# A fused layer norm, local attention and GeGLU kernel: three tiles transposed by DMA, late weights requested from GpSimd, the load order and a buffer count changed

## Chip, cores and metric

The kernel runs on one core of a Trainium2 chip. The metric is the device time of one execution in microseconds (us); it is given as a median over executions. One execution was also profiled, and its trace holds every instruction's start and end, in us from the start of the span.

## What is computed

The input x is 2048 rows of 512 numbers in bf16. Two branches read the same normalized rows, and their product is added back to x:

```python
xn = _layernorm(x, axis=-1)
s = _A_ref(xn, A_wqkv, A_wo)
g = _silu(_B_ref(xn, B_w_gate, B_w_up, B_w_down))
return x + s * g
```

Branch A is an attention of 32 heads of 16 numbers, in which position p sees only the eight positions p, p-2, ..., p-14; positions before the start are masked out. It ends in a product with wo (512 x 512). Branch B is a gated unit: gelu(xn w_gate) * (xn w_up) is multiplied by w_down, with an inner width of 1792.

## The kernel before

**Tiling.** The 2048 rows are 16 tiles of 128 rows (128 is the number of partitions), grouped in four chunks of four tiles: chunk 0 is tiles 0 to 3, chunk 1 tiles 4 to 7, and so on. All matmuls need the normalized rows with the 512 features on the partitions, so each normalized tile `xn` (L197 `normalize`) is transposed into `xnT` of its chunk. There are two ways to do that. `transpose` (L204) issues four TensorE transposes into a PSUM buffer, which ACT (or VectorE) copies to xnT. `transpose_by_dma` (L229) issues four DMA transposes of 128 x 128 from SP's queue.

**Stages.** For each chunk j the program runs three stages: `qkv` (L252; twelve blocks of 128 output features, four each of q, k and v), `glu` (L389; 14 steps fc, each with four matmuls into g_ps, four into u_ps, two evictions on ACT and the product h on VectorE) and `down` (L402; per tile 14 matmuls into y_ps with wd, four into s_ps with wo, and the closing product and sum). The order of program is: qkv of chunk 0, then for each chunk its glu, the qkv of the next chunk, and its down stage. The work of the attention is put between the steps of these stages: products of q and shifted k (`qk_product`, L285, VectorE), their sums (`logits`, L293, TensorE, with Exp on ACT and, for chunk 0, seven memsets of E on GpSimd), products with v (`av_product`, L353, VectorE; tile name pv), their sums (`av_sums`, L364, TensorE; o_ps), the denominators (L313), and the division (`divide`, L379, VectorE; oT).

**What sets the order.** The program is scheduled by hand. `at(key, fn, *args)` (L436) hangs a call on a step, and `run` (L439) issues the calls of a step ahead of it, in the order in which they were hung. Each engine then takes its own instructions strictly in program order, and waits on semaphores for what it needs from others. So a call's place fixes its place in each queue that it uses: TensorE (PE), VectorE (DVE), ScalarE (ACT), GpSimd (POOL), and SP, from which all DMAs of the kernel before are issued.

**Loads.** At the start SP requests x tiles 0 to 3 one by one, the q, k and v thirds of wqkv, then the rest of x between the halves of w_gate and w_up (L94 to L102). `load_late_weights` (L104) requests wd (w_down, 1792 KB) and wo (four requests of 128 KB). It hangs on step 0 of chunk 0's glu stage, behind the DMA transposes of tile 7 and `load_v` (L270; the four requests of v_arr for chunk 0, which read back from DRAM what the v blocks wrote there).

**Chunk 1's tiles.** Tiles 4 to 7 are normalized in chunk 0's qkv stage. Tiles 4, 5 and 6 are transposed on TensorE at steps 0, 1 and 2 of chunk 0's glu stage, and tile 7 by DMA. Chunk 1's qkv stage, which follows that glu stage, is the first to read them.

**Chunk 2's tiles.** Their statistics (`moments`, L187) come at steps 7 to 10 of that glu stage and their normalization at steps 8 to 11. `moments` ends with a power on GpSimd (L193, rstd to the power -0.5) that `normalize` waits for. Logits come at step 9, and the first two pv at steps 12 and 13.

**Buffers.** xn lives in pool `sm4`, four buffers per name. The PSUM pool `mm` has four buffers, which g_ps, u_ps, qkv_ps, y_ps, s_ps and the transposes' tr take in turn.

**Start.** Before x arrives, TensorE runs 17 matmuls of 256 columns on zeros (`warm_up`, L221), and twice four of 128 columns between the first transposes.

Of the kernel before, what the change touches and what calls it, by code (L numbers as in the profile page):

```python
# [10 lines left out]
BF16 = mybir.dt.bfloat16  # L11
F32 = mybir.dt.float32

P = 128
# [14 lines left out]
def kernel(  # L29
# [13 lines left out]
    nc = tc.nc  # L43
    B, S, D = A_x.shape
    DF = B_w_gate.shape[1]
    NT, NC, NF, NJ = S // P, D // P, DF // P, S // TQ
    TPQ = TQ // P
# [5 lines left out]
    def pool(name, bufs, **kw):  # L53
        return ctx.enter_context(tc.tile_pool(name=name, bufs=bufs, **kw))
# [11 lines left out]
    sm = pool("sm", 3)  # L66
    sm2 = pool("sm2", 2)
    sm4 = pool("sm4", 4)
    dram = pool("dram", 1, space=bass.MemoryType.DRAM)
    mm = pool("mm", 4, space=bass.MemoryType.PSUM)  # L70
    att = pool("att", 1, space=bass.MemoryType.PSUM)
# [3 lines left out]
    wqkv_sb = wts.tile([P, NC, 3 * D], BF16, name="wqkv_sb")  # L75
    wg_sb = wts.tile([P, NC, DF], BF16, name="wg_sb")
    wu_sb = wts.tile([P, NC, DF], BF16, name="wu_sb")
    wd_sb = wts.tile([P, NF, D], BF16, name="wd_sb")
# [4 lines left out]
    def load_x(t, n=1):  # L83
        nc.sync.dma_start(
            out=x_sb[:, t : t + n, :],
            in_=x2d[t * P : (t + n) * P, :].rearrange("(t p) d -> p t d", p=P),
        )

    def load_w(dst, src, lo, hi):
        nc.sync.dma_start(  # L90
            out=dst[:, :, lo:hi], in_=src.rearrange("(k p) n -> p k n", p=P)[:, :, lo:hi]
        )

    for t in range(TPQ):  # L94
        load_x(t)
    for i in range(3):
        load_w(wqkv_sb, A_wqkv, i * D, (i + 1) * D)
    load_x(TPQ, TPQ)
    for i, (lo, hi) in enumerate(((0, DF // 2), (DF // 2, DF))):
# [2 lines left out]
        load_x((2 + i) * TPQ, TPQ)  # L102

    def load_late_weights():  # L104
        nc.sync.dma_start(out=wd_sb[:], in_=B_w_down.rearrange("(k p) n -> p k n", p=P))
        for g in range(NC):
            nc.sync.dma_start(
                out=wo_sb[:, g, :],
                in_=bass.AP(
                    tensor=A_wo.tensor, offset=g * 4 * D, ap=[[D, 4], [DH * D, H], [1, D]]  # L110
                ),
            )
# [7 lines left out]
        out=vT.rearrange("(k p) n -> p k n", p=P)[:, :, 0:PAD],  # L120
        in_=warm[:, 0 : NC * PAD].rearrange("p (k n) -> p k n", k=NC),
# [54 lines left out]
    def first_moments(t):  # L176
        nc.vector.bn_stats(out=stats[:, t, :], in_=x_sb[:, t, :])  # L177
        nc.vector.bn_aggr(out=mv[:, t, :], in_=stats[:, t, :])
        nc.scalar.activation(
            out=std[:, t, :], in_=mv[:, t, 1:2], func=AF.Sqrt, bias=epsc[:], scale=1.0  # L180
        )

    def first_normalize(t):
        nc.vector.reciprocal(out=rstd[:, t, :], in_=std[:, t, :])
        normalize(t)
# [9 lines left out]
    xns = {}  # L195

    def normalize(t):  # L197
        xn = xns[t] = sm4.tile([P, D], BF16, name="xn")
        nc.vector.tensor_scalar(
            out=xn[:], in0=x_sb[:, t, :], scalar1=mv[:, t, 0:1], scalar2=rstd[:, t, :],  # L200
            op0=ALU.subtract, op1=ALU.mult,
        )
# [18 lines left out]
    def warm_up(n, cols):  # L221

        ps = mm.tile([P, TQ], F32, name="warm_ps", tag="mm")
        for _ in range(n):
            nc.tensor.matmul(
                ps[:, 0:cols], lhsT=warm[:, 0:P], rhs=warm[:, 0:cols], start=True, stop=True
            )
# [24 lines left out]
    def qkv(j, fo, i0=0, n=TQ, ps=None):  # L252
        which, c = divmod(fo, NC)
        if fo == 0 and i0 == 0:
            st[j]["q"] = qp.tile([P, NC, TQ], BF16, name="q_sb")
        if ps is None:
            ps = mm.tile([P, n], F32, name="qkv_ps", tag="mm")[:]
            project(ps, wqkv_sb, fo * P, j, i0, n)
        if which == 0:
            nc.scalar.activation(out=st[j]["q"][:, c, i0 : i0 + n], in_=ps, func=AF.Copy)  # L260
        elif which == 1:
            lo = PAD + j * TQ + i0
            nc.scalar.activation(out=k_sb[:, c, lo : lo + n], in_=ps, func=AF.Copy)  # L263
        else:
            vst = sm4.tile([P, TQ], BF16, name="vst")
            nc.scalar.activation(out=vst[:], in_=ps, func=AF.Copy)  # L266
            lo = PAD + j * TQ
            nc.sync.dma_start(out=vT[c * P : (c + 1) * P, lo : lo + TQ], in_=vst[:])
# [167 lines left out]
    def at(key, fn, *args):  # L436
        side.setdefault(key, []).append((fn, args))
# [5 lines left out]
    for i in range(TPQ):  # L443
        at(("qkv", 0, i), normalize, TPQ + i)
        at(("glu", 0, 7 + i), moments, 2 * TPQ + i)
        if i < TPQ - 1:
            at(("glu", 0, i), transpose, TPQ + i)
        at(("glu", 0, 8 + i), normalize, 2 * TPQ + i)
        at(("glu", 1, 0), transpose_by_dma, 2 * TPQ + i)
        at(("glu", 1, 10 + i), moments, 3 * TPQ + i)  # L450
        at(("qkv", 2, 2 * i), normalize, 3 * TPQ + i)
        at(("glu", 2, 0), transpose_by_dma, 3 * TPQ + i)
# [31 lines left out]
    HT = TPQ // 2  # L484
    HQ = HT * P
    warm_up(17, TQ // 2)
    first_moments(0)
    first_moments(1)
    first_normalize(0)
# [27 lines left out]
    for i in range(NC):  # L517
        run("qkv", 0, i)
        run("qkv", 0, NC + i)
        qkv(0, 2 * NC + i)  # L520
    at(("glu", 0, 0), transpose_by_dma, 2 * TPQ - 1)
    at(("glu", 0, 0), load_v, 0)
    at(("glu", 0, 0), load_late_weights)
    for j in range(NJ):
        for fc in range(NF):
            run("glu", j, fc)
# [36 lines left out]
```

The softmax here doesn't subtract the row's maximum and nothing guards it: scores larger than these inputs give would overflow.

## Time and profile before

| | us |
|---|---|
| median of 3 runs | 230.64 (230.31 to 230.83) |
| the profiled execution | 230.49 |
| its span, first to last instruction | 228.8 |
| PE busy | 222.7 |
| VectorE (DVE) busy | 147.6 |
| ScalarE (ACT) busy | 130.6 |
| GpSimd (POOL) busy | 21.7 |

The page of a profile gives the busy time of each engine and the chain of work that ended last, followed back from the last instruction. In a timeline, a line has the start and the time from the start of its first to the end of its last instruction, the engine, the line of the code, the operation, out<-in by the program's names, the shape and the count; in brackets stand the idle time of the engine before it and what released it. A matmul's end is modelled and overlaps the next, so PE is best read by starts. SPq is SP's issuing of DMAs: its time is that of the request, not of the data. L12 is line 12 of the kernel before; the changed kernel's lines stand up to six further down.

### The profile page before, as it was taken

The page shows a single profiled execution, that of the slowest core. Times are in us where ns is not written, and L with a number is a line of the kernel's source. Part 1 is how long each engine was busy: PE and PEld are TensorE (multiplying, and loading weights), DVE is VectorE, ACT ScalarE, POOL GpSimd, SP SyncE. Part 2 cuts the span into 40 slices and gives each one's busy share as a digit, 9 for nine tenths or more (in the row PEclk, how much of TensorE's full clock was granted, in tenths as well). Part 3 has the DMA queues.
Part 4 walks back from the last instruction along what each step waited for, and adds up shares of the span by engine and source line. Part 5 has one row for each costly group of instructions (what it writes and reads, how often), then busy time and mean ns, then how long its engine had stood idle before and what let it go on. Part 6 is the DMA issues. An engine that isn't in the chain of part 4 may idle for free.

```text
span 228.8 us, 3516 instructions
## 1 busy us (share of the span) xinstructions
PE 222.7 (97%) x1303; PEld 106.8 (47%) x1323; DVE 147.6 (65%) x234; ACT 130.6 (57%) x215; POOL 21.7 (10%) x61
## 2 busy tenths in 40 slices
PE   7999999999999999999999999999999999999994
PEld 5865444444444444444444444444444444444453
DVE  4593996894898198865678169735449429845232
ACT  3679779764514867476721687646741387647211
POOL 1048944100000000110000000000000000000000
PEclk9999999999999999999999999999999999999999
DMA  6999599922366611110266711110038910000001
GB/s 157 357 375 376 140 175 199 315 98 80 91 153 152 135 23 29 27 29 0 92 162 152 162 29 23 26 34 6 30 104 193 202 30 3 0 0 4 23 23 46
DMA packets 29857, 24.33 MB, mean 106 GB/s; under 512 B 9488, under 2 KB 29840, under 8 KB 29840
## 3 DMA queue, kind: packets, MB, share of 16 engines
q1 hardware_dynamic: 29840, 24.11, 41.0%
q8 instruction: 10, 0.16, 0.3%
q14 instruction: 7, 0.06, 0.1%
HBM read 18.61 MB, written 4.31 MB: 100 GB/s over the span
## 4 chain that ended last, share of the span: by engine, by line
PE 94%; ACT 2%; DVE 1%; DMA 1%; issue 1%; ACTq 0%; DVEq 0%
PE y_ps L411 21%; PE u_ps L242 21%; PE g_ps L242 20%; PE qkv_ps L242 17%; PE s_ps L421 6%; PE L_ps L299 3%; PE o_ps L370 3%; DMA x_sb<-in_A_x_dram 1%; PE q_ps L242 1%; PE tr L208 1%; DVE stats L177 1%; ACT L395 1%; ACT u L397 1%; PE den_ps L319 0%; ACT xnT L217 0%
## 5 line engine op out<-in xcount | busy, mean ns | idle before, releaser
L242 PE MATMUL u_ps<-xnT,wu_sb 128*128 128x512 bf16 x223 | 57.3, 379 | 0.2
L242 PE MATMUL g_ps<-xnT,wg_sb 128*128 128x512 bf16 x214 | 56.5, 379 | 0.6 <-issue 0.2
L411 PE MATMUL y_ps<-wd_sb,h 128*128 128x512 bf16 (+1 forms) x234 | 50.9, 366 | 0.2
L399 DVE TENSOR_TENSOR h<-ge,u 128x512 bf16<-128x512 bf16 x56 | 23.8, 424 | 37.5 <-ACT u L397 36.8
L288 DVE TENSOR_TENSOR pk<-q_sb,k_sb 128x2048 bf16<-128x2048 bf16 x32 | 37.8, 1221 | 7.0 <-ACT k_sb L263 7.0
L395 ACT ACTIVATE ge<-g_ps 128x512 bf16<-128x512 f32 x56 | 33.6, 600 | 14.7 <-PE g_ps L242 14.0
L397 ACT ACTIVATE u<-u_ps 128x512 bf16<-128x512 f32 x56 | 33.6, 599 | 14.6 <-PE u_ps L242 14.4
L242 PE MATMUL qkv_ps<-xnT,wqkv_sb 128*128 128x512 bf16 (+1 forms) x203 | 40.5, 354 | 0.2
L356 DVE TENSOR_TENSOR pv<-E,v_arr 128x2048 bf16<-128x2048 bf16 x32 | 38.6, 1217 | 0.0
L411 PEld LDWEIGHTS <-h 128*128 128x128 bf16 x238 | 23.3, 98 | 25.3
L418 ACT ACTIVATE sl<-y_ps 128x512 bf16<-128x512 f32 (+1 forms) x17 | 9.7, 573 | 44.0 <-PE y_ps L411 44.0
L242 PEld LDWEIGHTS <-wu_sb 128*128 128x128 bf16 x224 | 21.9, 98 | 26.6 <-issue 0.3
L242 PEld LDWEIGHTS <-wg_sb 128*128 128x128 bf16 x224 | 21.2, 98 | 26.8 <-issue 3.0
L242 PEld LDWEIGHTS <-wqkv_sb 128*128 128x128 bf16 x224 | 21.7, 98 | 19.6 <-issue 0.4
L429 DVE TENSOR_TENSOR m<-s_ps,sl 128x512 bf16<-128x512 f32 (+1 forms) x17 | 11.2, 658 | 22.4 <-PE s_ps L421 22.4
L421 PE MATMUL s_ps<-wo_sb,oT 128*128 128x512 bf16 (+1 forms) x68 | 16.6, 366 | 0.0
L193 POOL TENSOR_TENSOR rstd<-rstd,mhalf 128x1 f32<-128x1 f32 x12 | 7.7, 638 | 78.9 <-DVE rstd L190 76.7
L266 ACT ACTIVATE vst<-qkv_ps 128x512 bf16<-128x512 f32 x16 | 9.6, 598 | 6.4 <-PE qkv_ps L242 6.4
L263 ACT ACTIVATE k_sb<-qkv_ps 128x512 bf16<-128x512 f32 (+1 forms) x20 | 10.2, 517 | 3.4 <-PE qkv_ps L242 3.2
L260 ACT ACTIVATE q_sb<-qkv_ps 128x512 bf16<-128x512 f32 (+1 forms) x16 | 8.7, 545 | 3.5 <-PE qkv_ps L242 3.3
L421 PEld LDWEIGHTS <-oT 128*128 128x128 bf16 x68 | 6.6, 98 | 7.2
L382 DVE TENSOR_TENSOR oT<-o_ps,rbd 128x1024 bf16<-128x1024 f32 x6 | 7.1, 1219 | 3.7 <-PE qkv_ps L242 3.7
(52 smaller groups left out, 119.3 us busy)
## 6 DMA issues: line engine op xcount, KB each, us to landing
v_arr<-vT SPq DMA_DIRECT2D x16, 520.0 KB, 5.1
vT<-vst SPq DMA_DIRECT2D x16, 128.0 KB, 2.8
out_dram<-o_t SPq DMA_DIRECT2D x15, 128.0 KB, 2.3
wg_sb<-in_B_w_gate_dram SPq DMA_DIRECT2D x2, 896.0 KB, 10.8
wu_sb<-in_B_w_up_dram SPq DMA_DIRECT2D x2, 896.0 KB, 10.9
wd_sb<-in_B_w_down_dram SPq DMA_DIRECT2D x1, 1792.0 KB, 16.9
wqkv_sb<-in_A_wqkv_dram SPq DMA_DIRECT2D x3, 512.0 KB
x_sb<-in_A_x_dram SPq DMA_DIRECT2D x3, 512.0 KB, 11.6
```

The lines of the kernel that those rows point to most:

```text
L242: nc.tensor.matmul(ps, lhsT=w[:, dk, lo : lo + P], rhs=xnT[j][:, dk, i0 : i0 + n], start=(dk == 0), stop=(dk == NC - 1),)
L263: nc.scalar.activation(out=k_sb[:, c, lo : lo + n], in_=ps, func=AF.Copy)
L266: nc.scalar.activation(out=vst[:], in_=ps, func=AF.Copy)
L288: nc.vector.tensor_tensor(out=pk[:], in0=st[j]["q"][:], in1=k_sb[:, :, off : off + TQ], op=ALU.mult)
L356: nc.vector.tensor_tensor(out=pv[:], in0=st[j]["E"][:, wh, :].unsqueeze(1).to_broadcast([P, 4, TQ]), in1=st[j]["va"][:, 4 * g : 4 * g + 4, ...
L395: nc.scalar.activation(out=ge[:], in_=g_ps[:], func=AF.Gelu_apprx_tanh)
L397: nc.scalar.activation(out=u[:], in_=u_ps[:], func=AF.Copy)
L399: nc.vector.tensor_tensor(out=h[:], in0=ge[:], in1=u[:], op=ALU.mult)
L411: nc.tensor.matmul(y[:], lhsT=st[j][fc][:, tt * P : (tt + 1) * P], rhs=wd_sb[:, fc, cols], start=(fc == 0), stop=(fc == NF - 1),)
L418: nc.scalar.activation(out=sl[:, cols], in_=y[:], func=AF.Silu)
L421: nc.tensor.matmul(s[:], lhsT=st[j]["oT"][:, g, tt * P : (tt + 1) * P], rhs=wo_sb[:, g, cols], start=(g == 0), stop=(g == NC - 1),)
L429: nc.vector.tensor_tensor(out=m[:], in0=s[:], in1=sl[:, cols], op=ALU.mult)
```

## The change

Six edits. A pool `xnp` of six buffers holds xn. The q third of wqkv is requested ahead of x tile 3. wd and wo are requested from GpSimd's queue, and hang on step 9 of chunk 0's glu stage (behind that step's other calls, logits and its memsets of E among them) where they stood on step 0. Tile 4 alone is transposed on TensorE; tiles 5, 6 and 7 go by DMA at step 0, tile 5 ahead of `load_v` and tiles 6 and 7 behind it. Four warm-up matmuls of 128 columns follow the first 17.

```diff
+    xnp = pool("xnp", 6)
...
-    for t in range(TPQ):
+    for t in range(TPQ - 1):
         load_x(t)
-    for i in range(3):
+    load_w(wqkv_sb, A_wqkv, 0, D)
+    load_x(TPQ - 1)
+    for i in range(1, 3):
         load_w(wqkv_sb, A_wqkv, i * D, (i + 1) * D)
...
     def load_late_weights():
-        nc.sync.dma_start(out=wd_sb[:], in_=B_w_down.rearrange("(k p) n -> p k n", p=P))
+        nc.gpsimd.dma_start(out=wd_sb[:], in_=B_w_down.rearrange("(k p) n -> p k n", p=P))
         for g in range(NC):
-            nc.sync.dma_start(
+            nc.gpsimd.dma_start(
...
-        xn = xns[t] = sm4.tile([P, D], BF16, name="xn")
+        xn = xns[t] = xnp.tile([P, D], BF16, name="xn")
...
-        if i < TPQ - 1:
+        if i < 1:
             at(("glu", 0, i), transpose, TPQ + i)
...
     warm_up(17, TQ // 2)
+    warm_up(4, P)
...
-    at(("glu", 0, 0), transpose_by_dma, 2 * TPQ - 1)
+    at(("glu", 0, 0), transpose_by_dma, TPQ + 1)
     at(("glu", 0, 0), load_v, 0)
-    at(("glu", 0, 0), load_late_weights)
+    for t in range(TPQ + 2, 2 * TPQ):
+        at(("glu", 0, 0), transpose_by_dma, t)
+    at(("glu", 0, 9), load_late_weights)
```

## The prediction

> **What bounds the kernel now.** I read the page first: how busy each engine is, and the chain that ended last.
>
> ```profile
> PE 222.7 (97%) x1303; PEld 106.8 (47%) x1323; DVE 147.6 (65%) x234; ACT 130.6 (57%) x215; POOL 21.7 (10%) x61
> PE 94%; ACT 2%; DVE 1%; DMA 1%; issue 1%; ACTq 0%; DVEq 0%
> ```
>
> TensorE carries 94% of the chain, so a change can gain only by taking PE instructions away or closing one of its few gaps; whatever makes PE wait is lost, since later stages have no slack to win it back. Then the timeline of PE where chunk 0's gate/up stage begins, the first stage whose instructions the change takes away:
>
> ```profile
> 18.03 0.39 PE L208 MATMUL tr<-ident,xn 128*128 128x128 bf16 x4
> 18.25 1.03 PE L242 MATMUL g_ps<-xnT,wg_sb 128*128 128x512 bf16 x4
> 19.12 1.03 PE L242 MATMUL u_ps<-xnT,wu_sb 128*128 128x512 bf16 x4
> 19.98 0.39 PE L208 MATMUL tr<-ident,xn 128*128 128x128 bf16 x4
> 20.20 1.03 PE L242 MATMUL g_ps<-xnT,wg_sb 128*128 128x512 bf16 x4
> 21.28 1.02 PE L242 MATMUL u_ps<-xnT,wu_sb 128*128 128x512 bf16 x4
> 22.14 0.39 PE L208 MATMUL tr<-ident,xn 128*128 128x128 bf16 x4
> 24.09 0.38 PE L242 MATMUL g_ps<-xnT,wg_sb 128*128 128x512 bf16 x1
> ```
>
> Starts, not durations, give the pace: 0.22 us from a transposed tile (four transposes) to the next group, 0.86 to 0.87 for a group of four matmuls, but 1.08 from 20.20 to 21.28. The chain names the cause: the activation-table load on ACT (1.28 us from 19.34), then the first Gelu eviction to 21.24, which frees the PSUM buffer that the second u_ps takes.
>
> Third, GpSimd, VectorE, SP and PE from 27 to 58 us, where the moved requests will stand:
>
> ```profile
> 38.60 0.55 POOL L193 TENSOR_TENSOR rstd<-rstd,mhalf 128x1 f32<-128x1 f32 x1 [1.53 <-DVE rstd L190]
> 39.21 0.93 POOL L311 MEMSET E<- 32x2 bf16 x7
> 42.34 0.55 POOL L193 TENSOR_TENSOR rstd<-rstd,mhalf 128x1 f32<-128x1 f32 x1 [2.20 <-DVE h L399]
> ```
> ```profile
> 42.93 0.41 DVE L199 TENSOR_SCALAR xn<-x_sb,mv,rstd 128x512 bf16<-128x512 bf16 x1 [0.76 <-POOL rstd L193]
> 43.59 1.22 DVE L356 TENSOR_TENSOR pv<-E,v_arr 128x2048 bf16<-128x2048 bf16 x1
> 50.80 3.43 DVE L356 TENSOR_TENSOR pv<-E,v_arr 128x2048 bf16<-128x2048 bf16 x3
> 57.89 1.23 DVE L382 TENSOR_TENSOR oT<-o_ps,rbd 128x1024 bf16<-128x1024 f32 x1 [3.66 <-PE qkv_ps L242]
> ```
> ```profile
> 27.83 2.65 SPq L276 DMA_DIRECT2D v_arr<-vT  x4
> 30.53 0.67 SPq L105 DMA_DIRECT2D wd_sb<-in_B_w_down_dram  x1
> 31.24 14.42 SPq L107 DMA_DIRECT2D wo_sb<-in_A_wo_dram  x4
> ```
> ```profile
> 45.03 2.54 PE L242 MATMUL qkv_ps<-xnT,wqkv_sb 128*128 128x512 bf16 x11
> 54.09 1.91 PE L370 MATMUL o_ps<-pv,hsum 128*32 128x512 bf16 x32
> ```
>
> VectorE waits for GpSimd's power (tile 11's rstd) once already, at 42.93, and is then busy without a pause until pv ends at 54.23. GpSimd is idle 2.2 us between the memsets of E (end 40.14) and that power: the hole in which the change puts five DMA requests.
>
> **What the Trainium skill says.** *DMA: Bandwidth & Descriptors*, SWDGE vs HWDGE vs iDMA: requests from GpSimd have their descriptors written by software on its cores. Section Latency and other measured facts puts a first byte at about 1 us there ("the Q7 emission overhead") and 0.6 us from SP. No GpSimd request is in this trace; SP's accepted ones take 0.33 to 0.67 us. *TensorE: Matmul & The Clock Gate*, first table: GpSimd takes instructions strictly in order; the trace agrees as far as it goes. *DMA: Bandwidth & Descriptors*, Queues, rings and completion order: the engines alternate between queues packet by packet; no run here shows it, since nearly all data is SP's. *TensorE: Matmul & The Clock Gate*, What's actually happening: the clock doubles after one busy window of some 3.4 us. The trace agrees: 17 warm-up matmuls of 256 columns in 3.81 us, later 16 of the same size in 1.91.
>
> **The change part by part.**
>
> *Tiles 5 and 6 leave PE* (tile 7 went by DMA already). Two tiles x 0.22 us = 0.44. With the two PSUM buffers they took gone, the second g_ps and u_ps take buffers free by 19.4, and the third g_ps takes that of the first, free at 21.24 where PE would come at 18.25 + 4 x 0.864 = 21.71. So the 0.22 wait goes too. Check: 18.25 to 24.09 is 5.84; six groups are 5.18; **-0.66 us**. Next late would be PE's wait for the first u eviction (21.71, wanted at 22.57): covered. The two ACT copies (0.6 each) were beside PE: 0 more.
>
> *q weights ahead of x tile 3.* First q_ps at 7.15. xnT's first half is done about 7.04 and sets that; the weights landed at 6.88. They come earlier, behind three tiles, but xnT does not: **0**, up to -0.2 where the clock doubles before 6. The tile moved back must land before its statistics at 6.41 (landing 5.06 before); 0.5 MB at the 385 GB/s of that stretch is 1.4 us, partly in an emptier stretch, so about 6.3. If 0.5 late, xn of tiles 2 and 3 end near 8.5 and 9.1, where their transposes stand at 8.89 and 9.55: hidden.
>
> *Four more warm-up matmuls.* 4 x 0.107 (pace of the 128-column ones then) = 0.43 from 4.71 to 5.14, ahead of the transpose at 5.21, which waits for xn: **0**. Without that cover: up to +0.43; a clock that doubles a window earlier: some -0.3.
>
> *Six xn buffers.* Tile 11 takes tile 5's buffer instead of tile 7's; tile 5's transposes landed by 28.8, xn 11 comes at 42.9: **0**.
>
> *Tiles 5, 6, 7 by DMA.* Tile 5 takes tile 7's old place on SP (21.57 to 27.66), v_arr follows unchanged at 27.83, and eight transposes take the place of wd and wo. Each costs SP about 1.25 us. SP's requests rotate over eight semaphores, so tile 7's four wait for the four v_arr to land; the last landed 12.8 us after its issue at 29.86, i.e. 42.65. Its issue 1.23 plus 1.1 to landing (as tile 7's last: issued 26.43, landed 28.75) give 45.0. PE comes to that fourth matmul at 45.03 - 0.66 + 3 x 0.216 = 45.0. **0**, from 0 to +1.4: if the queues share, wd (1.8 MB at 342 GB/s, 5.3 us from 41.3) holds it to 46.6 at worst. Behind these on SP stand rs_d and rbd, ready at 50.9: nothing waits.
>
> *Late weights from GpSimd.* They stand behind the memsets of E and ahead of tile 11's power. Queued behind the power is VectorE's xn 11, and behind that h and all eight pv. Let G be the time of five requests on GpSimd. Power ends at 40.14 + G + 0.6, xn 11 starts G - 2.2 later than now (42.93), and as VectorE has no pause, pv ends that much after 54.23. PE needs the last pv at its 29th o_ps matmul, 54.09 + 28 x 0.049 = 55.47: slack 1.2 us. PE waits **G - 3.4** us if G is larger. This is in times of before; all engines here come 0.66 earlier together.
>
> G is the unknown. Below: SP's accepted issues, 0.67 + 4 x 0.33 = 2.0; or *SBUF — State Buffer*, A bandwidth-pool intuition that's wrong, 0.62 us for a lone GpSimd DMA, x 5 = 3.1. Above: what SP spent, 0.67 + 14.42 = 15.1[...]. I take 1.0 each, and 2.0 for wd, which has 14 rows a partition where wo has one: **G = 6.0**, an estimate, so +2.6. The data itself is early: wd would land about 48, wanted at 57.8; SP's 14.42 us of stalled wo issues hid behind nothing that waited, so their removal brings 0. VectorE is past this at its 3.66 us pause at 57.89, so the loss is paid once. Where PE also waits for a late transpose, the waits overlap: the larger counts.
>
> Sum: -0.66 + 2.6 = +1.9 on the profiled execution's 230.49 us (span 228.8 and 1.7 around it), 232.4. The median of three is 230.64, 0.15 above it; on that base **232.6**.
>
> **The rivals.**
>
> *A, forecast: VectorE held behind GpSimd's requests.* G from 4.5 to 9.4: 231.1 to 236.0, likeliest 232.6. For: in-order queue, no pause in VectorE from 42.93 to 54.23. Against: no GpSimd request has been timed here.
>
> *B, other side: short requests.* If G is under 3.4, they fit the 2.2 us hole and the 1.2 us slack, and only the removed transposes count: 230.64 - 0.66 = 230.0, 229.8 with a better start. It decides at G = 4.06; a measurable gain needs G below 3.6. For: SP's 0.33 to 0.67.
>
> *C: late transposes take the removed wait's place.* G short, tile 7's last transposes delayed behind wd's packets: -0.66 + 0.2 to 1.4 gives 230.2 to 231.4, middle 230.8. For: the 0.0 margin above. Against: a transpose is little data.
>
> *D: wd's many rows make G over 10,* as SP's own stall might hint: 237 and more.
>
> **How the numbers follow.** A 0.50, B 0.27, C 0.15, D 0.08. 0.2% is 0.46 us, about what a measurement of this kernel tells from no change. Faster: B, 0.27. Same: 0.09 of C and 0.02 at A's lower end, 0.11. Slower: 0.62. The range, 229.8 to 236.0, takes in B, C and A and leaves out D and tails. A's own is 231.1 to 236.0.
>
> **What would show it.** Right: first g_ps groups of chunk 0 0.86 us apart, with fc 3 5.2 us after fc 0; on GpSimd five requests between E's memsets and a power, and xn 11 on VectorE ending an idle time released by it, some 4 us late; PE idle at o_ps by G - 3.4. Wrong: xn 11 within 1.2 us of its place (B); PE idle at the first qkv_ps of chunk 1, released by a DMA into xnT (C); a first q_ps that moved from 7.15 by more than 0.2, or a PE wait at y_ps for wd, which I price at nothing.

## The result and the profile after

The changed kernel takes 238.25 us (median of 6 runs, 237.45 to 240.08), the kernel before 230.74 beside it (6 runs, 230.31 to 232.69): a ratio of 1.033, with a 95% interval of 1.027 to 1.039. It is slower, as forecast, but 2.25 us above the upper end of the range (236.0). The profiled execution took 237.55 us, with a span of 235.8 (before: 230.49 and 228.8).

First the page of the changed kernel: how busy PE is, and the shares of the chain that ended last.

```profile
PE 225.2 (95%) x1319; PEld 106.6 (45%) x1319; DVE 147.9 (63%) x234; ACT 129.7 (55%) x213; POOL 27.3 (12%) x66
PE 77%; DMA 14%; SPq 7%; issue 0%; DVE 0%; DVEq 0%
```

TensorE held 94% of the chain before; now DMA has 14% of it and SP's requests 7%. Part of that lies at the start (the page gives 5% to x_sb), but 5% is v_arr and 4% xnT: somewhere in the middle PE waited for a transfer. (More PE instructions are recorded than before although the change takes 8 transposes away and adds 4 matmuls: some records are missing from the trace of before, so instructions aren't counted here.)

The timeline of PE where chunk 0's gate/up stage begins comes next, the view that answers to the second one of the prediction. Columns: start, length of the group, engine, line, operation, out<-in, shape, count.

```profile
18.23 0.39 PE L211 MATMUL tr<-ident,xn 128*128 128x128 bf16 x4
18.45 1.03 PE L245 MATMUL g_ps<-xnT,wg_sb 128*128 128x512 bf16 x4
19.32 1.03 PE L245 MATMUL u_ps<-xnT,wu_sb 128*128 128x512 bf16 x4
...
23.63 1.03 PE L245 MATMUL g_ps<-xnT,wg_sb 128*128 128x512 bf16 x4
```

The groups stand 0.86 apart, and fc 3's g_ps comes 5.18 us after fc 0's, where it was 5.84: the 0.66 of the removed transposes and of the buffer wait is there in full. The stage began 0.20 later than before (18.25), so 0.46 of it is left.

The same view where chunk 1's qkv stage begins; in brackets the idle time of PE ahead of the line, and what ended it:

```profile
43.75 1.03 PE L245 MATMUL u_ps<-xnT,wu_sb 128*128 128x512 bf16 x4
45.07 0.81 PE L245 MATMUL qkv_ps<-xnT,wqkv_sb 128*128 128x512 bf16 x3 [0.29 <-DMA xnT<-xn]
50.88 3.57 PE L245 MATMUL qkv_ps<-xnT,wqkv_sb 128*128 128x512 bf16 x9 [5.00 <-DMA xnT<-xn]
54.38 0.29 PE L322 MATMUL den_ps<-E,hsum 128*32 128x128 bf16 x8
```

This is where the time went. The u_ps group's end, by starts, is 43.75 + 0.86 = 44.61; the first qkv_ps comes 0.46 later. Its fourth matmul (the fourth 128 features, dk 3) was due at 45.07 + 3 x 0.216 = 45.72 and comes at 50.88, 5.16 later. The chain says which transfer that was, in pieces in order of time:

```profile
29.68 12.87 DMA v_arr<-vT
42.55 0.02 issue
42.56 8.27 DMA xnT<-xn
50.83 0.04 issue
50.88 3.57 PE qkv_ps L245 x9
```

The last v_arr transfer lands at 42.55, as in the kernel before (42.65); its semaphore lets SP request the last transpose of tile 7 at 42.56; and this one takes 8.27 us to land. Its like in the kernel before took 2.3 (26.43 to 28.75).

GpSimd's queue at that time:

```profile
38.75 0.93 POOL L314 MEMSET E<- 32x2 bf16 x7
39.62 1.28 POOL L108 DMA_DIRECT2D wd_sb<-in_B_w_down_dram  x1
40.90 2.74 POOL L110 DMA_DIRECT2D wo_sb<-in_A_wo_dram  x4
43.71 0.56 POOL L196 TENSOR_TENSOR rstd<-rstd,mhalf 128x1 f32<-128x1 f32 x1
```

The five requests stand between E's memsets and the power, as the prediction said, and take 1.28 + 2.74 = 4.0 us, not 6.0. wd lands at 51.16, just beside the late transpose. VectorE's xn of tile 11 comes at 44.31, 1.38 later than before; as this stage ran 0.46 ahead, that is 1.84 behind its place, where "G - 2.2" gives 1.8. PE, which waits for the transpose, is held longer, so that this isn't felt.

The last part shows in a table of stretches: start and end, length, busy time of PE, PEld, DVE, ACT and POOL, granted clock, DMA share, GB/s.

```profile
44.00:46.00 2.00, 1.59 (x7) 0.49 (x6) 1.69 (x3) 1.15 (x2) 0.28 (x1) 1.00 1.01 319
46.00:48.00 2.00, 0.00 (x0) 0.00 (x0) 2.00 (x5) 0.00 (x0) 0.00 (x0) 1.00 1.05 353
48.00:50.00 2.00, 0.00 (x0) 0.00 (x0) 2.00 (x2) 0.00 (x0) 0.00 (x0) 1.00 1.22 277
50.50:53.50 3.00, 2.62 (x7) 0.95 (x7) 0.90 (x1) 0.89 (x2) 0.00 (x0) 0.50 0.60 101
```

While PE waits, the DMA engines move 277 to 353 GB/s; a transpose's 32 KB is little in that, so it is GpSimd's weights that they move. And when PE starts again its granted clock is 0.50: the trace has it halved from 50.46 to 53.87, 3.41 us. *TensorE: Matmul & The Clock Gate*, section What's actually happening, in the Trainium skill says that an idle window of some 3.4 us halves the clock until a busy window has passed; the trace agrees, with 5.00 us of waiting ahead of it. From dk 3 to den_ps is 3.50 us (50.88 to 54.38) where it was 2.03 (45.68 to 47.71): 1.47 more.

The sum by starts: +0.20 at the start, -0.66, +0.46, +5.16, +1.47 = +6.63. From there to the end each later stage of each chunk stands 6.66 us behind its place in the kernel before; nothing is won back and nothing more lost, up to VectorE's last product (226.37 before, 233.03 now). The span is 7.0 longer; the other 0.4 lies behind that product, where only the last transfers and the end of the program stand.

### The profile page after: what moved, and what is told of

Same layout as the page of the kernel before. It is cut to its first block, busy times and chain, and to the rows that moved or that the text cites. A ratio compares the mean times of both kernels' runs of the same rounds, so it can differ in the third digit from the quotient of the medians.

```text
span 235.8 us, 3535 instructions
## 1 busy us (share of the span) xinstructions
PE 225.2 (95%) x1319; PEld 106.6 (45%) x1319; DVE 147.9 (63%) x234; ACT 129.7 (55%) x213; POOL 27.3 (12%) x66
## 3 DMA queue, kind: packets, MB, share of 16 engines
q0 software_dynamic: 1040, 2.37, 4.0%
## 4 chain that ended last, share of the span: by engine, by line
PE 77%; DMA 14%; SPq 7%; issue 0%; DVE 0%; DVEq 0%
PE y_ps L414 21%; PE g_ps L245 16%; PE u_ps L245 15%; PE qkv_ps L245 14%; PE s_ps L424 6%; DMA v_arr<-vT 5%; DMA x_sb<-in_A_x_dram 5%; DMA xnT<-xn 4%; SPq L91 3%; PE o_ps L373 3%; PE L_ps L302 2%; SPq L85 2%; SPq L237 1%; SPq L279 1%; PE den_ps L322 0%
## 5 line engine op out<-in xcount | busy, mean ns | idle before, releaser
L245 PE MATMUL g_ps<-xnT,wg_sb 128*128 128x512 bf16 x224 | 57.5, 379 | 0.0
L245 PE MATMUL qkv_ps<-xnT,wqkv_sb 128*128 128x512 bf16 (+1 forms) x208 | 42.6, 363 | 5.3 <-DMA xnT<-xn 5.3
L158 POOL COPY spread<-ident 32x32 bf16<-32x32 bf16 x16 | 10.0, 663 | 0.2
```

Of the source, the lines that this page charges most:

```text
L158: nc.gpsimd.tensor_copy(out=spread[H * q : H * (q + 1), q, H * j : H * (j + 1)], in_=ident[H * q : H * (q + 1), H * q : H * (q + 1)],)
L245: nc.tensor.matmul(ps, lhsT=w[:, dk, lo : lo + P], rhs=xnT[j][:, dk, i0 : i0 + n], start=(dk == 0), stop=(dk == NC - 1),)
```

## The experiments

All kernels were compared with the kernel before on the same chip; its medians there were 230.51 to 230.66. "Offset" is the start of a PE stage in a kernel less its start in the kernel before. The expectations stand as they were recorded.

### Weights requested two steps later

```diff
-    at(("glu", 0, 9), load_late_weights)
+    at(("glu", 0, 11), load_late_weights)
```

> The changed kernel with the late weights still requested from GpSimd, but hung on step 11 of chunk 0's glu stage: behind tile 11's power instead of ahead of it, some 2.7 us later. Theory Q (the last DMA transpose of tile 7, issued only when the last v_arr has landed, comes to the DMA engines behind wd's rows and waits for them): it is now issued some 2 us ahead of wd's first data, lands about 45, and PE's wait at the fourth qkv_ps of chunk 1 falls from 5.2 us to under 1; the clock stays up; 230.3 to 231.2 us. Rival T (eight transposes behind v_arr are late by themselves, or a GpSimd request disturbs a transpose whenever it comes): the wait stays over 4 us, 237 or more. Step A of the prediction (VectorE held behind the requests): xn 11 is back within 0.3 us of its place.

Measured: 232.92 us (232.62 to 233.28), ratio 1.011 (1.009 to 1.012). The last transpose, requested at 43.15, lands at 45.71, and PE waits 0.60 at the first qkv_ps; the offset there is +0.15 in place of +6.66. So the wait came from the GpSimd requests ahead of it. But 1.7 us are lost later (offset +0.15 at y_ps, +1.87 after the first s_ps), which neither theory had foreseen. GpSimd's and PE's timelines of this kernel:

```profile
41.97 0.55 POOL L196 TENSOR_TENSOR rstd<-rstd,mhalf 128x1 f32<-128x1 f32 x1 [2.51 <-DVE h L402]
45.96 1.28 POOL L108 DMA_DIRECT2D wd_sb<-in_B_w_down_dram  x1 [3.44 <-issue]
```
```profile
61.84 0.60 PE L424 MATMUL s_ps<-wo_sb,oT 128*128 128x512 bf16 x2 [0.85 <-DVE oT L385]
62.98 0.61 PE L424 MATMUL s_ps<-wo_sb,oT 128*128 128x512 bf16 x2 [0.53 <-DVE oT L385]
```

GpSimd makes its request 3.44 us after the power ended, for a reason that the trace doesn't show. Then rs_d, which SP requests at 50.69, lands at 57.37 (6.7 us; 1.8 in the kernel before, 50.92 to 52.74); rbd, oT and s_ps follow late. rs_d is a plain copy of 32 KB. So it is not something about transposes alone: this copy, requested behind all of GpSimd's 2304 KB, was held as well.

### Two tiles by DMA, so that the last transpose is requested early

```diff
-        if i < 1:
+        if i < 2:
             at(("glu", 0, i), transpose, TPQ + i)
...
-    at(("glu", 0, 0), transpose_by_dma, TPQ + 1)
+    at(("glu", 0, 0), transpose_by_dma, TPQ + 2)
     at(("glu", 0, 0), load_v, 0)
-    for t in range(TPQ + 2, 2 * TPQ):
-        at(("glu", 0, 0), transpose_by_dma, t)
+    at(("glu", 0, 0), transpose_by_dma, 2 * TPQ - 1)
```

> The changed kernel with two tiles of chunk 1 by DMA (6 ahead of v_arr, 7 behind it) and tiles 4 and 5 on TensorE; weights from GpSimd at step 9 as in the change. Tile 7's four transposes then take semaphores that tile 6 freed and needn't wait for v_arr's landing: all are issued by about 36, ahead of wd. Theory Q: landed by 43 to 45, PE's wait under 0.5 us, what stays is step A (xn 11 late by 1.8 us, PE waiting some 0.6 at o_ps); 0.3 us less is saved than with three tiles: 230.5 to 231.5 us. Rival T (wd's data slows transposes that are already queued, or GpSimd's request does): a wait of 2 to 5 us at the first qkv_ps of chunk 1, 233 to 237.

Measured: 230.58 us (230.3 to 231.02), ratio 1.000 (0.9995 to 1.001). Tile 7's transposes are requested from 31.0 to 36.3, all before wd's request at 39.41, and land by 43.60; PE doesn't wait for them. What is left of the change then shows, in PE's timeline:

```profile
44.37 2.54 PE L245 MATMUL qkv_ps<-xnT,wqkv_sb 128*128 128x512 bf16 x11
...
55.45 0.40 PE L373 MATMUL o_ps<-pv,hsum 128*32 128x512 bf16 x4 [0.33 <-DVE pv L359]
```

The offset is -0.66 up to o_ps (-0.44 from the start, -0.22 for one tile that left PE) and -0.15 after it: the requests on GpSimd (1.28 + 2.73) cost 0.51 through power, xn and pv, where "G - 3.4" gives 0.6.

### Half of wd at step 9, the rest at step 11

```diff
...
-        nc.gpsimd.dma_start(out=wd_sb[:], in_=B_w_down.rearrange("(k p) n -> p k n", p=P))
+        load_wd(NF // 2, NF)
...
-    at(("glu", 0, 9), load_late_weights)
+    at(("glu", 0, 9), load_wd, 0, NF // 2)
+    at(("glu", 0, 11), load_late_weights)
```

`load_wd(lo, hi)` requests rows lo to hi of each partition's 14, from GpSimd; `load_late_weights` requests the second half and wo.

> The changed kernel with wd in two requests: rows 0 to 6 of each partition's 14 at step 9, the other seven and wo at step 11. Theory Q by amount (the transpose waits for the rows ahead of it): the engines carry 0.9 MB ahead of it, some 2.7 us, and the second half joins it, so it lands between 47 and 50 and PE waits 2 to 4.5 us: 233 to 236. If the wait is for a fixed number of rows that the engines took in ahead[...], the wait is some 4 us. Rival T (a GpSimd request in flight holds a transpose whatever its size): as in the change, 50.8 and 237 to 239.

Measured: 238.39 us (237.82 to 238.82), ratio 1.034 (1.032 to 1.037); half the rows at step 9 don't shorten it, as the other half was requested ahead of the last transpose too. The third transpose of tile 7 is requested at 39.05, 0.19 after the first half's request, and lands at 47.39 (the half: 47.15). The fourth is requested at 42.53, 0.70 after the second half's, and lands at 50.97 (the half: 50.84). PE's timeline shows a wait for each (the first, of 0.88, is for the transposes ahead of them):

```profile
44.91 0.59 PE L251 MATMUL qkv_ps<-xnT,wqkv_sb 128*128 128x512 bf16 x2 [0.88 <-DMA xnT<-xn]
47.43 0.38 PE L251 MATMUL qkv_ps<-xnT,wqkv_sb 128*128 128x512 bf16 x1 [1.92 <-DMA xnT<-xn]
51.01 3.57 PE L251 MATMUL qkv_ps<-xnT,wqkv_sb 128*128 128x512 bf16 x8 [3.21 <-DMA xnT<-xn]
```

### TensorE kept busy through the wait

```diff
         if j + 1 < NJ:
+            if j == 0:
+                warm_up(48, TQ // 2)
             for i in range(12):
```

> The changed kernel with 48 matmuls of 256 columns on zeros ahead of chunk 1's qkv stage (5.2 us at full clock, from 44.6 to 49.8), inside PE's wait. It adds work whose result isn't used. If 1.5 us of the loss is TensorE's half clock after its idle time (50.5 to 53.9 in the profile), that goes and the transpose's landing is untouched: some 1.5 us below the changed kernel in the profile, 236 to 237 us, and the runs lie closer together than 237.5 to 240.1. If the clock has no share: 238.2 as before, or above.

Measured: 236.19 us (236.04 to 236.94), ratio 1.025 (1.023 to 1.027). The last transpose is as late as in the changed kernel (51.71), but PE's clock stays up:

```profile
51.75 2.10 PE L245 MATMUL qkv_ps<-xnT,wqkv_sb 128*128 128x512 bf16 x8 [1.35 <-DMA xnT<-xn]
53.79 0.29 PE L322 MATMUL den_ps<-E,hsum 128*32 128x128 bf16 x8
```

From dk 3 to den_ps it is 2.04 us where the changed kernel has 3.50: the 1.47 was the clock.

### The kernel before, with the weights alone moved

The diff is against the kernel before.

```diff
-        nc.sync.dma_start(out=wd_sb[:], in_=B_w_down.rearrange("(k p) n -> p k n", p=P))
+        nc.gpsimd.dma_start(out=wd_sb[:], in_=B_w_down.rearrange("(k p) n -> p k n", p=P))
         for g in range(NC):
-            nc.sync.dma_start(
+            nc.gpsimd.dma_start(
...
-    at(("glu", 0, 0), load_late_weights)
+    at(("glu", 0, 9), load_late_weights)
```

> The kernel before with one edit of the change: late weights requested from GpSimd at step 9. Nothing waits on SP that could stand behind them there (tile 7's transposes landed by 28.8). Step A alone, with the measured length of the five requests, 4.0 us: xn 11 starts 1.8 us late, PE waits 0.6 us at o_ps (4.0 - 3.4), 231.0 to 231.4 us. Theory Q adds only that rs_d, asked for at 52.7 now, may come behind wo: 0 to 0.5 more. If a GpSimd request costs by its mere presence (rival T): well above 232.

Measured: 231.39 us (231.35 to 231.56), ratio 1.0037 (1.0025 to 1.0049). xn of tile 11 waits 1.98 for the power, PE waits 0.33 at o_ps, and the offset goes from +0.18 (the start of this run) to +0.69 at o_ps: 0.51, the same as with two tiles by DMA. No SP request that is wanted soon stands behind the weights, and there is no 5 us wait. So GpSimd's queue alone doesn't make it; it takes a small request from SP that comes after the weights.

### The kernel before, with the two start edits alone

The diff is against the kernel before.

```diff
-    for t in range(TPQ):
+    for t in range(TPQ - 1):
         load_x(t)
-    for i in range(3):
+    load_w(wqkv_sb, A_wqkv, 0, D)
+    load_x(TPQ - 1)
+    for i in range(1, 3):
...
     warm_up(17, TQ // 2)
+    warm_up(4, P)
```

> The kernel before with the two start edits: q weights ahead of x tile 3, four more warm-up matmuls. The forecast was 0, up to -0.2. In the runs so far that hold these edits, the first q_ps stood +0.11, -0.01, -0.44, -0.55 and -0.08 us from its old place, so the mean is -0.2: 230.3 to 230.6 us, within 0.2% of before. If the start edits had a share in the loss: above 231.

Measured: 230.28 us (229.96 to 230.48), ratio 0.9985 (0.9977 to 0.9993). The offset is -0.21 at q_ps and at every stage after it.

### Two tiles by DMA, wo two steps later

The kernel with two tiles by DMA, and:

```diff
-    at(("glu", 0, 9), load_late_weights)
+    at(("glu", 0, 9), load_wd)
+    at(("glu", 0, 11), load_wo)
```

(`load_wd` and `load_wo` are the two parts of `load_late_weights`, both from GpSimd.)

> Two tiles by DMA (tiles 6 and 7, as in the run with two), wd requested from GpSimd at step 9 and the four wo at step 11, behind tile 11's power. wd's request (1.28 us) fits GpSimd's 2.2 us hole, so xn 11 is back in place and PE's 0.5 us wait at o_ps goes; wo's data still ends by 52, as wd's data sets it. Theory Q: rs_d, asked for at about 50.3, lands behind wo's last rows, at 52 to 54, with some 2 us of slack before s_ps. 230.58 - 0.5 gives 229.9 to 230.3 us. If rs_d comes behind wo by more than that: PE waits at the first s_ps, 230.6 to 232.

Measured: 230.04 us (229.83 to 230.74), ratio 0.9981 (0.9972 to 0.9989). VectorE's idle time ahead of xn 11 shrinks to 0.46:

```profile
42.75 0.41 DVE L204 TENSOR_SCALAR xn<-x_sb,mv,rstd 128x512 bf16<-128x512 bf16 x1 [0.46 <-POOL rstd L198]
```

PE no longer waits at o_ps, and the offset of -0.48 after the first stages (-0.25 from the start, the rest for the one tile that left PE) is still there at the end. rs_d, requested at 50.74, lands at 52.48, in 1.75 us: wd had landed at 50.27, and wo's last part did at 52.32. Its median is the lowest of the study, and its interval stays below 1: a gain of 0.2%.

### v_arr between the transposes of tile 6

```diff
     at(("glu", 0, 0), transpose_by_dma, TPQ + 1)
+    at(("glu", 0, 0), transpose_by_dma, TPQ + 2, (0, 1))
     at(("glu", 0, 0), load_v, 0)
-    for t in range(TPQ + 2, 2 * TPQ):
-        at(("glu", 0, 0), transpose_by_dma, t)
+    at(("glu", 0, 0), transpose_by_dma, TPQ + 2, (2, 3))
+    at(("glu", 0, 0), transpose_by_dma, 2 * TPQ - 1)
```

(`transpose_by_dma` takes the blocks of 128 features to transpose as its second argument.)

> The changed kernel with one difference: v_arr's four requests stand between the second and third transposes of tile 6 rather than ahead of tile 6. Tile 7's last transpose then waits for the landing of the second v_arr (about 38) and not of the fourth (42.6), so it is issued by 41, ahead of the bulk of wd's data; v_arr is issued 2.5 us later and lands about 45. Theory Q with the semaphore rotation as the trigger: no wait of 5 us at the fourth qkv_ps; xn 11 late by 1.8 and pv by 1.6 (one cover for both), PE waits some 0.5 to 1 at o_ps; 230.4 to 231.6 us. Rival (three tiles by DMA are too many whatever their order): 234 or more.

Measured: 238.08 us (236.56 to 238.58), ratio 1.032 (1.030 to 1.035). It was meant to have the last transpose requested ahead of wd, and missed that by half a microsecond: wd's request begins at 38.94, the transpose's at 39.48; it lands at 49.47. PE waits 2.04 (for transposes that came with a later v_arr) and 2.19, and its clock is halved for 6.83 us, from 46.45:

```profile
46.15 1.18 PE L245 MATMUL qkv_ps<-xnT,wqkv_sb 128*128 128x512 bf16 x3 [2.04 <-DMA xnT<-xn]
49.51 3.95 PE L245 MATMUL qkv_ps<-xnT,wqkv_sb 128*128 128x512 bf16 x9 [2.19 <-DMA xnT<-xn]
```

That fits a delay set by the order of the requests in time, but does not show it: the transpose landed 3.2 us ahead of wd (52.69) here, and v_arr had moved as well.

### The weights back on SP, at the same step

```diff
-        nc.gpsimd.dma_start(out=wd_sb[:], in_=B_w_down.rearrange("(k p) n -> p k n", p=P))
+        nc.sync.dma_start(out=wd_sb[:], in_=B_w_down.rearrange("(k p) n -> p k n", p=P))
         for g in range(NC):
-            nc.gpsimd.dma_start(
+            nc.sync.dma_start(
```

> The changed kernel with the five late weight requests back on SP's queue, still on step 9, so that they stand behind all the transposes and v_arr. Theory W (an SP request that comes after a GpSimd request lands only with that one's data): no GpSimd request is left, so tile 7's last transpose, requested about 42.6, lands about 45.0, PE waits under 0.6 us at chunk 1's first qkv_ps, the clock stays up; -0.66 for the removed transposes remains. The weights then go out from about 43.7 on, and rs_d, requested from about 50.7, can stand behind wo's data on SP; that costs 0 to 2 us at s_ps. 230.0 to 232.0. Rival P (the place alone: the last transpose is late because it stands behind v_arr, whoever requests the weights): the wait of 5 us at qkv_ps stays, 236 to 238.

Measured: 232.72 us (232.42 to 233.14), ratio 1.009 (1.007 to 1.011). Everything else is the changed kernel, the last transpose again waits for v_arr (requested at 42.71), and lands at 45.26, where the prediction had 45.0. PE's timeline:

```profile
44.73 2.54 PE L245 MATMUL qkv_ps<-xnT,wqkv_sb 128*128 128x512 bf16 x11 [0.18 <-DMA xnT<-xn]
...
61.92 0.61 PE L424 MATMUL s_ps<-wo_sb,oT 128*128 128x512 bf16 x2 [1.37 <-DVE oT L385]
63.05 0.60 PE L424 MATMUL s_ps<-wo_sb,oT 128*128 128x512 bf16 x2 [0.53 <-DVE oT L385]
```

The place of the transpose behind v_arr costs 0.18; the rival that blamed the place falls. What is lost here is lost later: rs_d, requested at 50.60, stands behind wd and wo on SP's own queue, lands at 57.46, and s_ps waits for it (offset -0.30 before, +1.94 after). Its semaphore tells more: 12 of its 16 increments came by 53.00, the last four from 57.27 to 57.46. wo's requests, which from GpSimd landed in 16 increments each, end in four late ones each on SP, the last from 57.10 to 57.28. So it is the end of wo, rather than wd (landed at 51.80), that rs_d came in with.

### wo first, wd two steps later

```diff
     at(("glu", 0, 9), load_late_weights)
+    at(("glu", 0, 11), load_wd)
```

(`load_late_weights` requests wo alone here, and `load_wd` requests wd from GpSimd.)

> The changed kernel with wo's four requests (512 KB) alone on GpSimd at step 9 and wd's one request (1792 KB) from GpSimd at step 11. Tile 7's last transpose, requested about 42.6, then has 512 KB requested by GpSimd ahead of it where it had 2304. Theory S (what it waits for is the data ahead of it, so the size counts): it lands between 45.0 and 47.0, PE waits 0.3 to 2.0 us at qkv_ps; wd, later, holds rs_d as in the kernel that had all late weights at step 11, which costs about 2 us at s_ps and o_ps: 231.0 to 234.0. Rival F (a fixed delay behind any GpSimd request, whatever its size): it lands about 50.8 again, and the time is 236.5 to 239.

Measured: 237.12 us (236.46 to 238.6), ratio 1.030 (1.026 to 1.034). With wo's 512 KB ahead of it the last transpose, requested at 42.49, lands at 48.74 (wo's last part: 48.50), 6.25 us later, where it was 8.27 behind wd and most of wo. The landing is between the two expectations. The excess over some 2.5 us is still 65% (3.75 of 5.77), but wd's request follows the transpose's by 0.38, and how much of the excess is wd's was not separated. PE's timeline:

```profile
45.44 0.81 PE L247 MATMUL qkv_ps<-xnT,wqkv_sb 128*128 128x512 bf16 x3 [0.90 <-DMA xnT<-xn]
48.78 3.57 PE L247 MATMUL qkv_ps<-xnT,wqkv_sb 128*128 128x512 bf16 x8 [2.53 <-DMA xnT<-xn]
```

It goes to half clock again, for 6.83 us, which puts the time nearer to the rival's.

### v_arr behind all transposes

```diff
...
-    at(("glu", 0, 0), load_v, 0)
     for t in range(TPQ + 2, 2 * TPQ):
         at(("glu", 0, 0), transpose_by_dma, t)
-    at(("glu", 0, 9), load_late_weights)
+    at(("glu", 0, 0), load_v, 0)
+    at(("glu", 0, 9), load_wd)
+    at(("glu", 0, 11), load_wo)
```

> The changed kernel with v_arr's four requests behind all twelve transposes instead of behind tile 5's, and with wd on step 9, the four wo on step 11 of GpSimd's calls. Theory W: tile 7's transposes are requested before 36.5, ahead of every GpSimd request, and land before 40; PE doesn't wait at qkv_ps. v_arr is requested from about 36 to 39.5, ahead of wd's request (about 39.4) or just at it: if it lands by 43.5, the pv start in their place and the time is 229.6 to 230.4. Rival V (v_arr's rows take 12 us from request to landing wherever they stand, or fall behind wd's request): v_arr lands at 46 to 49, the pv and with them PE at o_ps come 2 to 5 us late, 232 to 235.

Measured: 249.01 us (248.01 to 249.37), ratio 1.079 (1.076 to 1.082), the slowest of all, far beyond both expectations. The transposes are in by 40.5. The four v_arr are requested at 38.97, 39.68, 40.34 and 41.08, wd at 38.84: the first of them lands at 44.75, the others at 54.41, 58.14 and 60.54. VectorE waits for the last:

```profile
60.76 1.22 DVE L361 TENSOR_TENSOR pv<-E,v_arr 128x2048 bf16<-128x2048 bf16 x1 [18.00 <-DMA v_arr<-vT]
```

The delay moved with the requests that came after GpSimd's. The packets show why so much: from 45.5 to 49.5 wd and v_arr moved 252 and 250 of them, equal turns, but a packet of wd has 4096 bytes and one of v_arr 1040. PE then waited for the pv one after another, and its clock was halved from 55.93 for 20.5 us, which has its share in the 18.4 us.

### wo from GpSimd early, wd on SP at the end

```diff
-        nc.gpsimd.dma_start(out=wd_sb[:], in_=B_w_down.rearrange("(k p) n -> p k n", p=P))
+        nc.sync.dma_start(out=wd_sb[:], in_=B_w_down.rearrange("(k p) n -> p k n", p=P))
...
-    at(("glu", 0, 9), load_late_weights)
+    at(("glu", 0, 0), load_wo)
+    at(("glu", 0, 9), load_wd)
```

> A version made from the findings: the changed kernel with wo's four requests from GpSimd at step 0 (in its queue they then stand behind the last constant it builds, so from about 30.1, just after v_arr's four requests on SP at 27.6 to 30.3) and wd's one request on SP behind tile 7's last transpose (about 43.7). Theory W (what SP requests after a GpSimd request lands with that one's data, what it requested before does not wait): v_arr is ahead of wo's requests and lands about 42.6 as before; tile 6's and 7's transposes are behind 512 KB only, which is in by 40; tile 7's last lands about 45.3, wait under 0.6; wd lands about 52 and rs_d, behind it alone, by 53, early enough for the division at 56.7. The gain of the removed transposes is kept: 229.7 to 230.4. Rival V (v_arr, still under way when wo's data moves, is late by wo's 1.5 us or more, and with it tile 7's last transpose and the pv): PE waits 1 to 2 us at qkv_ps, 231.0 to 232.5.

Measured: 235.47 us (233.33 to 236.3), ratio 1.020 (1.017 to 1.023). A version built on the findings so far, and it failed. wo is requested from 31.66 to 34.56; v_arr on SP from 29.33 to 32.00, that is 1.7 us later than in the changed kernel and hardly ahead of wo. The first three v_arr land at 34.77, 37.33 and 41.61; the fourth, requested 0.28 before wo, lands at 46.88 with wo's last part (46.80). The transposes behind it land from 47.34 on, tile 7's first at 48.18, and PE waits for that one:

```profile
48.32 1.90 PE L247 MATMUL qkv_ps<-xnT,wqkv_sb 128*128 128x512 bf16 x5 [4.07 <-DMA xnT<-xn]
```

The last transpose, requested at 46.90 when its semaphore came free, lands at 49.17; the clock is halved from 49.25 for 3.41 us. So it is not the moment of the request that protects: v_arr's data takes long to move (11.0 us in the changed kernel, 29.07 to 40.07), its last part was still under way when wo's first packets moved at 38.28, and the packets of both moved side by side until 45.5. Why v_arr was requested 1.7 late in this run isn't shown.

## Why the prediction was right or wrong

**Sign right by luck, size wrong.** The likeliest case had slower for another reason (VectorE held behind GpSimd). That reason costs 0.51 where it stands alone, less than the 0.66 won, so by itself it would not have made the kernel slower. The case that named the true mechanism (C) put it at 1.4 us at most.

**The step that failed** is "Tiles 5, 6, 7 by DMA", at **0**, from 0 to +1.4, "holds it to 46.6 at worst". Its first half was right: the rotation of semaphores makes tile 7's last transpose wait for the last v_arr, whose landing was put at 42.65 (42.55 measured), and without GpSimd's requests it lands at 45.26 for 45.0 (weights back on SP). The worst case failed: behind wd it landed at 50.83. (46.6 less 45.0 is 1.6, not the 1.4 of the sum; either is far too little.) The bound let wd's data move from 41.3 on, for 5.3 us. The trace has the first wd packets at 42.69, 3.1 us after the request, 30 of 448 before 44, and wd landed at 51.16. The transpose, for all its small size, landed only 0.33 before it, 4.2 us behind the bound. Measured for the step: 0.46 + 5.16 of waiting.

What the runs show of that wait is this. Each row is an SP transfer, and the GpSimd request, if any, that had begun before it:

| kernel | SP's transfer, requested | GpSimd's request ahead | landed | that one landed |
|---|---|---|---|---|
| changed | tile 7's third, 38.54 | none (wd 39.62) | 45.37 | |
| changed | tile 7's fourth, 42.56 | wd 39.62 | 50.83 | 51.16 |
| weights at step 11 | fourth, 43.15 | none (wd 45.96) | 45.71 | |
| weights at step 11 | rs_d, 50.69 | wd 45.96, wo | 57.37 | 56.16, 58.08 |
| half of wd | third, 39.05 | half 38.86 | 47.39 | 47.15 |
| half of wd | fourth, 42.53 | half 41.83 | 50.97 | 50.84 |
| kept busy | fourth, 43.17 | wd 39.34 | 51.71 | 51.47 |
| v_arr between | fourth, 39.48 | wd 38.94 | 49.47 | 52.69 |
| weights on SP | fourth, 42.71 | none at all | 45.26 | |
| wo first | fourth, 42.49 | wo 39.38 | 48.74 | 48.50 |

In six of the seven rows with a GpSimd request ahead, the transfer landed within 0.33 us of that one, or between its landings; with v_arr between, it landed 3.2 us earlier. It took 6.3 to 10.0 us from its own request. Without one ahead the fourth takes 2.6 and rs_d 1.8. The third stands behind v_arr's data and takes 6.83 even so; so do the third with half of wd and the fourth with v_arr between, whose excess is smaller than 2.5 would make it. Two cases bound the rule: in the kernel with v_arr last, the first v_arr, requested 0.13 us after wd's request began, landed in 5.8 us, ahead of it; and in the kernel with wo early a request made 0.28 before GpSimd's was held, as three more of v_arr's stood ahead of it on SP's queue.

**How the engines do it** the packets show in part. In the changed kernel, the transpose's 128 packets of 256 bytes begin to move only at 47.37, 4.8 us after the request, when 300 of wd's 448 packets of 4096 bytes had begun; then the two take turns, with 124 of wd's and 114 of the transpose's from 47.5 to 49.0. The Trainium skill, *DMA: Bandwidth & Descriptors*, section Queues, rings and completion order, says that an engine drains a whole packet of 9 to 17 descriptors from one queue before it turns to another. The trace agrees as to the turns; why they began so late is not explained by it and stays open. The same section says that a semaphore's write lands only after every earlier write of that engine, from whichever queue. That fits the landings at 47.39 and 50.97, beside GpSimd's own, and the third transpose with half of wd, whose packets had moved by 43.44 and whose semaphore writes came from 46.28 on, with those of the half. The prediction took from that section only that engines alternate, and so gave a small transfer a quick turn.

Which part weighs how much can be read for the last transpose, against its like with the weights at step 11 (8.27 us in all for 2.56):

| us | changed | weights at step 11 |
|---|---|---|
| request to its first packet | 4.81 | 1.11 |
| first to last packet | 1.65 | 0.29 |
| last packet to landing | 1.81 | 1.16 |

So 5.1 of the 5.7 us are late and slow packets. For the third transpose with half of wd it is the other way about: its packets were through 3.95 us ahead of its landing.

**A cost no case had**: half clock after the wait, 1.47, shown by the kernel that keeps PE busy. The prediction cited the page for the start of the kernel and didn't ask what a wait in the middle would do. The kernels that waited 0.2 to 0.6 us there kept the clock, and so did the one kept busy, with a wait of 1.35. With v_arr between it was halved at 46.45, when PE had waited once, for 2.04 us, and had been at work again for 0.30: a wait shorter than the page's window was enough.

**Tiles 5 and 6 leave PE**, -0.66: right; -0.65 to -0.66 in every kernel with three tiles by DMA.

**Late weights from GpSimd**: G was 4.0 for an estimate of 6.0 (1.28 for wd, 0.68 to 0.73 for each wo, where 2.0 and 1.0 were taken). "G - 3.4" gives 0.6, measured 0.51 alone and with two tiles; the trace of before has the 29th o_ps matmul start at 55.61 for the prediction's 55.47, which makes it G - 3.5. In the changed kernel it is hidden under PE's longer wait, as the prediction had it for two waits at once. So even without the transposes the forecast's +2.6 would have been 2 too much, and the case of short requests (B, decided at G = 4.06) lay at its border.

**The start edits**, 0 to -0.2: -0.21 alone. In the changed kernel's profiled execution the first q_ps came at 7.26 for 7.15, because the q weights landed at 7.21, later than before (6.88), although they were requested earlier. x tile 3, moved back, landed at 7.59 where about 6.3 was expected, and the stages that follow began 0.20 late. In the eleven other kernels with the same start the first q_ps came earlier than in the kernel before, at 6.57 to 7.13. Where the clock doubled near 4 us (with two tiles by DMA: 4.20, wo two steps later: 4.05, half of wd: 3.98) it came at 6.60 to 6.80, and at 7.07 and 7.13 where it doubled at 6.40 and 6.93: so in a single execution the prediction's "clock that doubles before 6" goes with up to 0.6, not 0.2. These are single executions, and the runs show no gain of that size for the start edits alone (ratio 0.9985).

**Six buffers**, 0: nothing shows against it. The trace names a transfer of xnT as what released xn 11, but tile 5's transposes, which free its buffer, had landed by 29.25, and the power it waits for ended at 44.27, just before 44.31.

**"Behind these on SP stand rs_d and rbd ... nothing waits"**: right for the changed kernel (rs_d came late itself, at 55.71), and no general truth: two experiments lost 1.7 and 2.2 us just there.

**Open**: why GpSimd's request came 3.44 us late at step 11 of the first experiment, and why the turns of the transpose's packets began so late. The spread of the changed kernel's runs (237.45 at a mean clock of 0.992, 240.08 at 0.979) goes with the clock; that the slower ones have a longer stretch at half clock, as three experiments did (6.83 us), is likely and not shown.

## What to carry to other kernels

A bulk load moved to another queue is not out of the way of a small transfer on the first one: in these runs the packets of both took turns, and a small transfer requested after the bulk one mostly landed beside it. So place a bulk request where nothing is requested after it that is wanted within its duration (here 10 us), and where no earlier load is still under way; follow each semaphore chain to see what is requested late. When a wait in the middle of a matmul stream may reach 2 us or more, price the half clock after it as well (1.5 us here), and when a bound is meant as the worst case, let the competing transfer end first, with its own late start.

## What the runs showed of the hardware that was not expected

- In the changed kernel a request from GpSimd holds it 1.28 us for wd (1792 rows of 1 KB) and 0.68 to 0.73 for 128 rows; half of wd's rows took 1.17 and 1.02. wd's first packets moved 3.1 us after its request began, and 2.0 after it at step 11, where nothing else was moving; 10 to 14 us passed from request to landing.
- v_arr, four times 520 KB in packets of 1040 bytes, moves at about 190 GB/s with the engines' time filled; wd, in packets of 4096, at 319 and 353 GB/s in the stretches from 44 to 48. What came behind v_arr, from SP or from GpSimd, waited for it: in the kernel with wo early, wo's first packets moved 6.6 us after its first request.
- The same wo ends in four late increments a request from SP, in 16 from GpSimd. With the weights on SP, the engines moved some 94 GB/s from 53 to 56, when little but wo was left, and its last part landed at 57.28.
- One wait of 2.04 us was enough to halve PE's clock, for 6.83 us (v_arr between); waits of 0.60 (weights at step 11) and 1.35 (kept busy) left it alone.
